# One 33-row matmul in place of two one-row matmuls in the first expert's weight fold

## The chip, the cores and the metric
The kernel runs on one core of one Trainium2 chip. The metric is the device time of one execution in microseconds (us); the time before is the median of three runs. The engines are PE (matrix multiply; PEld is its weight load), DVE (vector), ACT (scalar), POOL (GpSimd) and SP, which here issues the transfers.

## The reference
Two batches of 3008 x 256 go through a two-dimensional Fourier transform, of which the real part is kept; the 6016 rows that come out go through two experts of width 2048, the first with the SiLU activation, the second with a leaky ramp.

```python
X = np.fft.fft(x, axis=1)
X = np.fft.fft(X, axis=2)
x = X.real.astype(np.float32).reshape(6016, 256)
h = x @ w_in;  g = h * (1.0 / (1.0 + np.exp(-h)))
x = g @ w_out                                          # first expert
h = x @ w_in2; g = np.maximum(h, 0) + alpha * np.minimum(h, 0)
return g @ w_out2                                      # second expert
```

## The kernel before
The transform along the 256 columns is not done on the data. It is folded into the first expert's input weights: each of four groups g of 512 weight columns is made ready in two halves h, and in each half sums and differences of weight rows are multiplied by a cosine and a sine table. The products with the table rows take full precision by splitting numbers: a value is held as a high part, which the engine's rounded float keeps exactly, and a low part, the rest.

The half h of a group g goes through seven steps in `prep_w1`. `total` and `rest` (DVE, L436 and L439) form sums and differences in a tile `we`, 256 columns each: the left half is called even, the right half odd. `high` (ACT, L442) copies all 512 columns to `WI[1, g, 2h]`, rounded. `low` (DVE, L446) subtracts that from `we` and writes the low part to `WI[1, g, 2h + 1]`. `fold` (PE, L459) issues eight matmuls of 256 columns into one PSUM bank `cw`: five for the even output (cosine table high times even high and even low, cosine table low times even high, and two more for the odd row) and three for the odd output. The two for the odd row have one partition each: row 0 of the odd half, high and then low, against a table row `OD0` that holds 0, 1, 0, 1, ... . `fold_high` (ACT, L469) and `fold_low` (DVE, L475) read the bank back into `WI`, split again.

Group 0 is made in an opening section whose order on every engine is written out by hand. Groups 1 to 3 are made inside the main loop of the first expert, while it already runs: the dictionary `PLAN` gives the iterations in which their steps are traced (i1 and f1 for group 1, and so on; i holds the steps up to `low`, f those from `fold` on). In that part the order of instructions in each engine's queue is chosen when the program is built, by a list scheduler that simulates the engines' times; `leash` holds the planned steps of an iteration behind named instructions of the iterations just before it on the same engine. The last part, the second expert, again has an order written by hand.

An iteration of the main loop multiplies the transformed data by 128 weight columns. `eo_half` (PE, L627 to L629) makes `pe` and `po`, three matmuls of 502 columns each; DVE adds and subtracts them (`t` at L642, `hp` at L645, `t` at L646); ACT takes the SiLU twice for each (L651, L652); POOL or DVE makes the low part (L664); and three iterations later `mm2` (PE, L686 to L690) multiplies by the output weights. `pe`, `po` and the fold's `cw` all come out of one pool of four PSUM banks, taken in turn: a bank of `po` is free again after L646, a bank of `cw` after L475. A second pool of four banks holds the sums of `mm2`, which ACT (L699) and DVE (L697, L695) carry out when a pass over a block ends.

Of the kernel before, what the change touches and what calls it, by code (L numbers as in the profile page):

```python
# [9 lines left out]
F32 = mybir.dt.float32  # L10
F32R = mybir.dt.float32r
# [60 lines left out]
def _tables():  # L72
    c = np.zeros((128, NCONST), np.float64)
    n1 = np.arange(N1)
    th = 2 * np.pi * np.outer(n1, np.arange(33)) / N1
    fa = np.zeros((N1, 64))
    fa[:, :32] = np.cos(th[:, :32])
    fa[:, 32] = np.cos(th[:, 32])
    fa[:, 33:] = np.sin(th[:, 1:32])
    fr = fa.copy()  # L80
    fr[:, 1:32] = -fa[:, 33:]
    fr[:, 33:] = fa[:, 1:32]
    for q in range(2):
        for j in range(2):
            for k0, k1 in zip(K_PARTS, K_PARTS[1:]):
                at = 4 * k0 + (2 * q + j) * (k1 - k0)
                for to, f in ((FA0, fa), (FR0, fr)):
                    c[64 * q : 64 * q + 64, to + at : to + at + k1 - k0] = f[:, 32 * j + k0 : 32 * j + k1]
    n2 = np.arange(24)
    ph = 2 * np.pi * np.outer(n2, np.arange(N2)) / N2  # L90
    co, si = np.cos(ph), np.sin(ph)
    row = 4 * (n2 % 12) + 2 * (n2 // 12)
    for h, (re, im) in enumerate(((co, -si), (si, co))):
        for j in range(2):
            for to, at in ((R0 + 94 * h, 47 * j), (RS0 + 95 * h, 48 if j else None)):
                if at is None:
                    c[row, to : to + 24] = re[:, :24]
                    c[row + 1, to + 24 : to + 48] = re[:, :24]
                else:
                    c[48 * j + row, to + at : to + at + 47] = re  # L100
                    c[48 * j + row + 1, to + at : to + at + 47] = im
    m = np.arange(128)
    ps = 2 * np.pi * np.outer(m, m) / D
    c[:, CD0 : CD0 + 128] = np.cos(ps)
    c[0, CD0 : CD0 + 128] = c[:, CD0] = 1 - m % 2
    c[:, SD0 : SD0 + 128] = -np.sin(ps)
    c[0, SG0 : SG0 + 128] = 1
    c[:, OC0 : OC0 + 2] = (m % 2)[:, None]
    c[0, OD0 : OD0 + 128] = m % 2
    return c.astype(np.float32)  # L110


# [11 lines left out]
def fft_moe_kernel(  # L124
# [32 lines left out]
    def mm_ps(name, w=512):  # L157
        return pm.tile([128, w], F32, tag="mm", name=name)
# [234 lines left out]
    WS = {}  # L393
    RAW = {}
    TOP = []

    def load_part(key, src, at, o, w):

# [25 lines left out]
    def prep_w1(g):  # L424

        pieces = []

        def steps(h, v):
            t = []
            ps = []  # L430

            def total(eng):
                if h == 0:
                    wi_tiles(1, g)
                t.append(conv(F32, f"we{g}_{h}"))
                eng.tensor_tensor(t[0][:, :256], v[0][:, :256], v[0][:, 256:], op=ALU.add)  # L436

            def rest(eng):
                eng.tensor_tensor(t[0][:, 256:], v[0][:, :256], v[0][:, 256:], op=ALU.subtract)  # L439

            def high():
                nc.scalar.activation(WI[1, g, 2 * h], t[0], AF.Copy)  # L442

            def low(eng):
                hi, lo = WI[1, g, 2 * h], WI[1, g, 2 * h + 1]
                eng.tensor_tensor(lo, t[0], hi.bitcast(F32), op=ALU.subtract)  # L446

            def fold():
                e, o = ([WI[1, g, 2 * h + j][:, at : at + 256] for j in range(2)] for at in (0, 256))
                ps.append(mm_ps(f"cw{g}_{h}"))  # L450
                runs = (
                    ((ch, CD0, e[0]), (ch, CD0, e[1]), (cl, CD0, e[0]), (ch, OD0, o[0]), (ch, OD0, o[1])),
                    ((ch, SD0, o[0]), (ch, SD0, o[1]), (cl, SD0, o[0])),
                )
                for k, run_ in enumerate(runs):
                    for j, (w, at, x) in enumerate(run_):
                        w = w[:, at - CD0 : at - CD0 + 128]
                        to = ps[0][:, 256 * k : 256 * k + 256]
                        nc.tensor.matmul(to, w, x, start=j == 0, stop=j == len(run_) - 1)  # L459
                if g:  # L460
                    return
                ps.append(acc_ps(f"r{g}_{h}", 4))
                for q in range(2):
                    for j in range(2):
                        w = e[j][:, 128 * q : 128 * q + 128]
                        nc.tensor.matmul(ps[1][:, 2 * q : 2 * q + 2], w, co, start=j == 0, stop=j == 1)

            def fold_high():
                nc.scalar.activation(WI[1, g, 2 * h], ps[0], AF.Copy)  # L469
                if g == 0:  # L470
                    nc.scalar.activation(odd_sb[:, 2 * h : 2 * h + 2], ps[1][:, ::2], AF.Copy)

            def fold_low():
                hi, lo = WI[1, g, 2 * h], WI[1, g, 2 * h + 1]
                nc.vector.tensor_tensor(lo, ps[0], hi.bitcast(F32), op=ALU.subtract)  # L475

            return [lambda: total(nc.vector), lambda: rest(nc.vector), high, (lambda: low(nc.vector)), fold, fold_high, fold_low]

        for h in range(2):
            v, st = to_f32(None, (f"i{g}", 512 * h, 512), f"i{g}_{h}")  # L480
            pieces.append((st, steps(h, v)))
        return pieces
# [392 lines left out]
    if True:  # L875
        with tc.manual_schedule():
            zero = conv(F32, "zero")
            nc.vector.memset(zero[:, :256], 0.0)
            warm(zero[:, :128], zero[:, :256], WARM0)
            for j in range(2):  # L880
                TOP.append(xp.tile([128, 512], U32, tag="xs", name=f"top{j}"))
                nc.gpsimd.memset(TOP[j].bitcast(F32), 0.0)
            nc.vector.memset(sm, 0.0)
            nc.scalar.activation(sm[:1, :1], sm[:1, :1], AF.Silu)
            for j in range(len(PIECES) - 1):
                load_x(0, j, (PIECES[j + 1] - PIECES[j]) // 2)
                if j == 0:
                    nc.sync.dma_start(cs[:, :R0], cst[:, :R0])
            cc = conv(F32, "cc")
            load_half("i0", wi1, 0)  # L890
            nc.sync.dma_start(cc, cst[:, CD0:])
            load_half("i0", wi1, 1)
            nc.sync.dma_start(cs[:, R0:], cst[:, R0:CD0])
            fold, mm, rest = stage_a(0)
            (i00, post0), (i01, post1) = prep_w1(0)
            post0, post1 = ([s if callable(s) else s[1] for s in p] for p in (post0, post1))
            for (h, i), n in zip(A_ORDER, A_WARM):
                if h == 0:
                    run(fold(i))
                mm(h, i)  # L900
                warm(cs[:, FA0 : FA0 + 128], cs[:, :256], n)
            for h in range(2):
                load_y(0, h, 0)
            load_half("o0", wo1, 0)
            rest(1)
            load_half("o0", wo1, 1)
            for h in range(2):
                load_y(0, h, 1)
            rest(2)
            load_w1(1)  # L910
            for h in range(2):
                load_y(0, h, 2)
            load_o1(1)
            nc.sync.dma_start(alpha_sb, alpha)
            (s0, p0), (s1, p1) = prep_o1(0)
            warm(cs[:, FA0 : FA0 + 128], cs[:, :256], WARM[0])
            run(i00[:1])
            nc.scalar.activation(ch, cc, AF.Copy)
            run(i00[1:])
            run(post0[:2])  # L920
            nc.vector.tensor_tensor(cl, cc[:, : SG0 - CD0], ch.bitcast(F32)[:, : SG0 - CD0], op=ALU.subtract)
            nc.gpsimd.tensor_copy(co, cs[:, OC0 : OC0 + 2])
            run(post0[2:4])
            run(i01)
            run(post1[:2])
            run(post0[4:5])
            warm(cs[:, FA0 : FA0 + 128], cs[:, :256], WARM[1])
            run(post0[5:])
            run(post1[2:4])
            warm(cs[:, FA0 : FA0 + 128], cs[:, :256], WARM[2])  # L930
            b00, b01 = stage_b(0, 0), stage_b(0, 1)
            run(b00[:2])
            run(b01[:2])
            run(s0)
            ps0 = eo_mm(0, lambda: first_row(0, 0))
            run(post1[4:5])
            ps1 = eo_mm(1)
            run(p0[:1])
            silu_split(0, *ps0, between=lambda: run(post1[5:]))
            run(p0[1:])  # L940
            silu_split(1, *ps1)
# [181 lines left out]
```

## Time and profile before

| what | value |
|---|---|
| median of three runs | 949.72 us (949.55 to 949.81) |
| the profiled execution | 950.28 us, of which the span from first to last instruction is 947.9 us |
| PE busy | 938.3 us (99%) |
| DVE, ACT, POOL busy | 740.9 us (78%), 709.2 us (75%), 368.5 us (39%) |
| granted TensorE clock, mean | 0.999 of 2.4 GHz |

A busy share says how much of the span an engine had an instruction under way; PE's matmuls overlap in it, so a matmul's own duration is longer than the step to the next one. Where an engine sat idle, the trace names what ended the wait; that name is inferred from the last event before the start.

### The profile page before, as it was taken

How to read it: one execution, taken by the hardware profiler on the slowest of the kernel's cores; microseconds unless marked ns; L12 is line 12 of the kernel's file. 1: busy time of each engine (PE TensorE's matmuls, PEld its weight loads, DVE VectorE, ACT ScalarE, POOL GpSimd, SP SyncE). 2: the span in 40 equal slices, each digit the busy share in tenths (PEclk: the TensorE clock that was granted, in tenths of full speed). 3: DMA queues.
4: the chain of work that ended last, by engine and by line, in shares of the span. 5: the costliest groups of instructions: out<-in, count | busy, mean ns of one | idle time of the engine just before them, and what ended most of it. 6: DMA issues, size and time to landing. Idle time of an engine off the chain costs nothing.

```text
span 947.9 us, 14357 instructions
## 1 busy us (share of the span) xinstructions
PE 938.3 (99%) x5188; PEld 816.0 (86%) x5188; DVE 740.9 (78%) x1277; ACT 709.2 (75%) x1398; POOL 368.5 (39%) x324
## 2 busy tenths in 40 slices
PE   8999999999999999999999999999999999999997
PEld 5888888888888888888899999999999999999996
DVE  5898988977756566786988788787888878788876
ACT  4777776755766676776978888787888878788875
POOL 2356658732466666876422122121212212121200
PEclk9999999999999999999999999999999999999999
DMA  8730300134303311100200200020020002000000
GB/s 270 266 99 22 131 28 23 67 82 143 124 1 117 133 59 42 44 1 1 87 22 2 66 1 23 1 67 22 1 66 1 22 2 66 23 1 22 1 23 22
DMA packets 18638, 51.98 MB, mean 55 GB/s; under 512 B 1924, under 2 KB 11912, under 8 KB 16392
## 3 DMA queue, kind: packets, MB, share of 16 engines
q1 hardware_dynamic: 18568, 51.08, 16.0%
q8 instruction: 40, 0.66, 0.3%
q14 instruction: 30, 0.25, 0.1%
HBM read 35.58 MB, written 15.49 MB: 54 GB/s over the span
## 4 chain that ended last, share of the span: by engine, by line
PE 95%; DVE 2%; ACT 1%; issue 1%; DMA 0%; POOL 0%; SPq 0%; ACTq 0%; DVEq 0%
PE a L858 27%; PE ac L760 21%; PE a L686 9%; PE a L688 9%; PE a L690 9%; PE b L760 3%; PE pe L627 2%; PE pe L629 2%; PE pe L628 2%; PE po L629 2%; PE po L628 2%; PE po L627 2%; PE psb L338 1%; PE psa L284 1%; PE cw L459 1%
## 5 line engine op out<-in xcount | busy, mean ns | idle before, releaser
L858 PE MATMUL a<-gh,wo 128*128 128x502 f32 x768 | 267.7, 390 | 0.0
L858 PEld LDWEIGHTS a<-gh,wo 128*128 128x128 f32 x768 | 144.7, 188 | 22.7
L664 POOL TENSOR_TENSOR gl<-t,gh 128x502 fp32r<-128x502 f32 x96 | 126.8, 1321 | 81.5 <-ACT t L652 66.4
L827 DVE SCALAR_TENSOR_TENSOR h<-h,fc,q 128x502 f32<-128x502 f32 x192 | 125.0, 651 | 34.4 <-ACT q L822 30.3
L858 PE MATMUL a<-gl,wo 128*128 128x502 f32 x384 | 149.5, 390 | 0.0
L838 DVE TENSOR_TENSOR gl<-h,gh 128x502 fp32r<-128x502 f32 x192 | 144.9, 755 | 0.1
L651 ACT ACTIVATE gh<-hp 128x502 fp32r<-128x502 f32 x96 | 59.8, 623 | 98.8 <-DVE hp L645 97.3
L688 PE MATMUL a<-gl,wo 128*128 128x502 f32 x384 | 129.9, 391 | 0.0
L690 PE MATMUL a<-gh,wo 128*128 128x502 f32 x384 | 128.1, 390 | 0.0
L686 PE MATMUL a<-gh,wo 128*128 128x502 f32 x384 | 125.0, 391 | 0.0
L833 ACT ACTIVATE gh<-h 128x502 fp32r<-128x502 f32 x192 | 118.4, 617 | 2.2 <-DVE h L827 2.1
L822 ACT ACTIVATE q<-h,fc 128x502 f32<-128x502 f32 x192 | 116.8, 609 | 2.8 <-DVE h L805 1.5
L664 POOL TENSOR_TENSOR gl<-hp,gh 128x502 fp32r<-128x502 f32 x63 | 81.5, 1294 | 81.5 <-ACT hp L652 72.5
L642 DVE SCALAR_TENSOR_TENSOR t<-n,sm,pe 128x502 f32<-128x502 f32 x96 | 70.3, 732 | 48.5 <-PE pe L629 40.1
L690 PEld LDWEIGHTS a<-gh,wo 128*128 128x128 f32 x384 | 72.4, 189 | 15.0
L688 PEld LDWEIGHTS a<-gl,wo 128*128 128x128 f32 x384 | 72.3, 189 | 14.9
L746 POOL TENSOR_TENSOR os<-o1r,os 128x252 fp32r<-128x252 f32 x36 | 33.1, 930 | 132.4 <-ACT os L745 132.4
L686 PEld LDWEIGHTS a<-gh,wo 128*128 128x128 f32 x384 | 71.8, 189 | 14.2
L858 PEld LDWEIGHTS a<-gl,wo 128*128 128x128 f32 x384 | 72.4, 188 | 7.7
L794 ACT ACTIVATE u<-ac 128x252 f32<-128x252 f32 x96 | 36.6, 382 | 54.2 <-PE ac L760 54.1
L736 POOL TENSOR_TENSOR xt<-o1r 128x252 f32<-128x252 f32 x24 | 17.4, 728 | 153.8 <-DVE h L827 150.2
L645 DVE TENSOR_TENSOR hp<-t,po 128x502 f32<-128x502 f32 x96 | 64.6, 673 | 14.2 <-PE po L629 9.6
(162 smaller groups left out, 2187.8 us busy)
## 6 DMA issues: line engine op xcount, KB each, us to landing
od<-o SPq DMA_DIRECT2D x6, 1004.0 KB, 4.3
o1r<-od SPq DMA_DIRECT2D x6, 1004.0 KB, 5.7
out_t<-ot SPq DMA_DIRECT2D x24, 251.0 KB, 2.6
x<-in_xs SPq DMA_DIRECT2D x8, 512.0 KB, 6.5
raw_w<-in_wi SPq DMA_DIRECT2D x4, 1024.0 KB, 8.0
raw_w<-in_wo SPq DMA_DIRECT2D x4, 1024.0 KB, 7.5
raw_i<-in_wi SPq DMA_DIRECT2D x3, 1024.0 KB, 5.8
raw_o<-in_wo SPq DMA_DIRECT2D x3, 1024.0 KB, 6.7
```

What stands on the lines that cost most here:

```text
L642: nc.vector.scalar_tensor_tensor(t, E128[c], odd_sb[:, f : f + 1], pe, op0=ALU.mult, op1=ALU.add)
L645: nc.vector.tensor_tensor(hp, t, po, op=ALU.add)
L664: LAST["gl", i] = (nc.gpsimd if s or lo_pool(i + 1) else nc.vector).tensor_tensor(lo, h, hi.bitcast(F32), op=ALU.subtract)
L686: nc.tensor.matmul(ACC1[lb, s], hi, G[i, s][0], start=st, stop=False)
L688: nc.tensor.matmul(ACC1[lb, s], hi, G[i, s][1], start=False, stop=False)
L690: nc.tensor.matmul(ACC1[lb, s], lo, G[i, s][0], start=False, stop=sp)
L760: nc.tensor.matmul(to, w, x, start=start and q == 0, stop=q == 2, skip_group_check=True)
L822: nc.scalar.activation(h["q", i][:, to], source(n, part), AF.Abs, scale=coef(n, i, 1))
L827: nc.vector.scalar_tensor_tensor(h[f"h{i}"][:, to], source(n, part), coef(n, i, 0), h["q", i][:, to], op0=ALU.mult, op1=ALU.add)
L833: nc.scalar.activation(hi, H[n][f"h{i}"], AF.Copy)
L838: nc.vector.tensor_tensor(lo, H[n][f"h{i}"], G[n, i][0].bitcast(F32), op=ALU.subtract)
L858: nc.tensor.matmul(ACC2[lb], w[lb][j], x, start=st and first, stop=sp and last)
```

## The change
For groups 1 to 3 the two one-row matmuls become one matmul of 33 rows. Two new tiles `PAIR` (33 partitions x 256, one for each half h, kept for the whole kernel) hold the high part of the odd row in partition 0 and its low part in partition 32; the rows between are zero. The table row `OD0` is repeated in partition 32 of the constants. `high` gets a second ACT copy of one partition x 256, `low` a second DVE subtraction of one partition x 256, both written to `PAIR`; both are done six times. The two tiles are set to zero by POOL at the start. Group 0 keeps its two matmuls.

```diff
@@ _tables
-    c[0, OD0 : OD0 + 128] = m % 2
+    c[0, OD0 : OD0 + 128] = c[32, OD0 : OD0 + 128] = m % 2
@@ fft_moe_kernel
     TOP = []
+    PAIR = []
@@ prep_w1
             def high():
                 nc.scalar.activation(WI[1, g, 2 * h], t[0], AF.Copy)
+                if g:
+                    nc.scalar.activation(PAIR[h][:1], t[0][:1, 256:], AF.Copy)
 
             def low(eng):
                 hi, lo = WI[1, g, 2 * h], WI[1, g, 2 * h + 1]
                 eng.tensor_tensor(lo, t[0], hi.bitcast(F32), op=ALU.subtract)
+                if g:
+                    eng.tensor_tensor(PAIR[h][32:33], t[0][:1, 256:], hi.bitcast(F32)[:1, 256:], op=ALU.subtract)
 
             def fold():
                 e, o = ([WI[1, g, 2 * h + j][:, at : at + 256] for j in range(2)] for at in (0, 256))
                 ps.append(mm_ps(f"cw{g}_{h}"))
+                if g:
+                    first = ((ch[:33], OD0, PAIR[h]),)
+                else:
+                    first = ((ch[:1], OD0, o[0][:1]), (ch[:1], OD0, o[1][:1]))
                 runs = (
-                    ((ch, CD0, e[0]), (ch, CD0, e[1]), (cl, CD0, e[0]), (ch, OD0, o[0]), (ch, OD0, o[1])),
+                    ((ch, CD0, e[0]), (ch, CD0, e[1]), (cl, CD0, e[0]), *first),
                     ((ch, SD0, o[0]), (ch, SD0, o[1]), (cl, SD0, o[0])),
                 )
@@ the opening section
             for j in range(2):
                 TOP.append(xp.tile([128, 512], U32, tag="xs", name=f"top{j}"))
                 nc.gpsimd.memset(TOP[j].bitcast(F32), 0.0)
+                PAIR.append(wp.tile([33, 256], F32R, name=f"pair{j}"))
+                nc.gpsimd.memset(PAIR[j].bitcast(F32), 0.0)
```

## Rows read from the trace of the kernel before

**Rows 1.** The profile's first part: busy time, share of the span, instructions.
```profile
PE 938.3 (99%) x5188; PEld 816.0 (86%) x5188; DVE 740.9 (78%) x1277; ACT 709.2 (75%) x1398; POOL 368.5 (39%) x324
```

**Rows 2.** Who PE waited for, whole span; in total, times, longest.
```profile
PE cw L459 <- ACT wi L442: 0.5, 1, 0.5
PE cw L459 <- ACT o L699: 0.5, 1, 0.5
PE cw L459 <- DVE wi L446: 0.3, 1, 0.3
```

**Rows 3.** Busy time by engine from 30 to 155 us: stretch, length, busy.
```profile
30.00:155.00 125.00, 124.53 (x591) 104.42 (x589) 110.44 (x161) 93.74 (x167) 76.56 (x60) 1.00 0.27 92
```

**Rows 4.** PE in order of time: start, us; first fold matmul, first instruction after.
```profile
139.86 0.40 PE L459 MATMUL cw<-wi,ch 128*128 128x256 f32 x2
...
140.79 0.39 PE L686 MATMUL a<-gh,wo 128*128 128x502 f32 x1
```

**Rows 5.** The fold's line, 60 to 150 us: duration min/median/max in ns.
```profile
L459 PE MATMUL cw<-wi,ch x36: 277/280/356, 65.8 to 146.1; 128*128 128x256 f32 x36
```

**Rows 6.** DVE on the tile we, all groups: duration min/median/max in ns.
```profile
L436 DVE TENSOR_TENSOR we<-cvi x8: 418/664/1504, 18.4 to 135.3; 128x256 f32<-128x256 f32 x8
L439 DVE TENSOR_TENSOR we<-cvi x8: 411/417/419, 18.7 to 136.1; 128x256 f32<-128x256 f32 x8
...
L446 DVE TENSOR_TENSOR wi<-we,wi x8: 679/776/1486, 19.9 to 137.8; 128x512 fp32r<-128x512 f32 x8
```

**Rows 7.** DVE groups by shape: busy us, mean ns; the narrowest subtraction.
```profile
L358 DVE TENSOR_TENSOR z<-psb,z 128x63 fp32r<-128x63 f32 x4 | 0.9, 214 | 0.0
```

**Rows 8.** DVE in order of time, three instructions without a wait between them.
```profile
92.47 0.42 DVE L436 TENSOR_TENSOR we<-cvi 128x256 f32<-128x256 f32 x1
92.80 0.42 DVE L439 TENSOR_TENSOR we<-cvi 128x256 f32<-128x256 f32 x1
93.14 0.73 DVE L642 SCALAR_TENSOR_TENSOR t<-n,sm,pe 128x502 f32<-128x502 f32 x1
```

**Rows 9.** ACT groups by shape: busy us, mean ns.
```profile
L169 ACT ACTIVATE xr<-x 128x256 fp32r<-128x256 f32 x4 | 1.6, 403 | 0.0
...
L884 ACT ACTIVATE sm<-sm 1x1 f32<-1x1 f32 x1 | 0.2, 202 | 0.0
```

**Rows 10.** All engines in order of time around group 1's second fold; idle in brackets.
```profile
64.15 1.41 DVE L446 TENSOR_TENSOR wi<-we,wi 128x512 fp32r<-128x512 f32 x1 [0.93 <-ACT wi L442]
...
65.30 0.63 ACT L652 ACTIVATE hp<-hp 128x502 f32<-128x502 f32 x1
...
65.48 0.67 DVE L646 TENSOR_TENSOR t<-t,po 128x502 f32<-128x502 f32 x1
...
66.00 1.27 POOL L664 TENSOR_TENSOR gl<-hp,gh 128x502 fp32r<-128x502 f32 x1 [0.99 <-ACT hp L652]
...
66.07 1.75 DVE L194 SCALAR_TENSOR_TENSOR cvt<-raw_t,top 128x512 uint32<-128x512 uint32 x1
...
70.13 0.39 PE L629 MATMUL po<-z,wi 128*128 128x502 f32 x1
70.18 0.66 DVE L646 TENSOR_TENSOR t<-t,po 128x502 f32<-128x502 f32 x1
70.27 0.57 ACT L699 ACTIVATE o<-a 128x502 f32<-128x502 f32 x1
...
70.99 0.47 PE L459 MATMUL cw<-wi,ch 128*128 128x256 f32 x2 [0.47 <-ACT o L699]
```

**Rows 11.** All engines in order of time around group 2's second fold.
```profile
115.76 0.66 DVE L646 TENSOR_TENSOR t<-t,po 128x502 f32<-128x502 f32 x1
...
118.62 0.40 PE L459 MATMUL cw<-wi,ch 128*128 128x256 f32 x2
```

**Rows 12.** POOL in order of time at the start; idle before in brackets.
```profile
0.71 0.99 POOL L882 MEMSET top<- 128x512 f32 x2 [0.29 <-POOLq L1105]
6.65 1.77 POOL L256 TENSOR_TENSOR x<-x 128x512 f32<-128x512 f32 x1 [4.95 <-DVE x L256]
```

## The prediction, made before the changed kernel was run
> **What bounds the kernel now.** I read the profile's first part, then PE's list of waits, then the stage in which the edit lies, and last the instructions around the edit in order of time. The first part shows PE busy for 938.3 of 947.9 us, with DVE next at 740.9 [rows 1]: time is PE's, and a change pays only in matmul time removed or in waits of PE. Of the waits that concern the fold there are three [rows 2]; two of them (on L442 and on L446) are group 0's, in the opening section, which the edit leaves alone. The third, 0.47 us, is in group 1's second half. The groups that change are made between 30 and 155 us, and there PE is busy 124.53 of 125.00 us: the missing 0.47 is this one wait. But DVE is busy 110.44 us in it and ACT 93.74 [rows 3], so DVE, which gets extra work, has 14.6 us free in the stage, far less headroom than its 78% of the whole span suggests.
>
> The wait itself: PE issues the last `po` matmul at 70.13 and the fold's first at 70.99, 0.47 us idle [rows 10]. The trace names ACT's L699, which ends at 70.27 + 0.57 = 70.84. DVE's L646 also ends at 70.18 + 0.66 = 70.84. The code decides: L699 frees a bank of the other pool, which the fold does not use, whereas L646 gives back the `po` bank that `cw` needs as the next of four. So PE waited for DVE, and DVE ran from 64.15 with no idle gap of note, one instruction behind another.
>
> **What the change removes.** Six matmuls with their weight loads. A fold is eight matmuls of one shape; from its first to the next instruction's start is 140.79 - 139.86 = 0.93 us [rows 4], so 0.116 us each. The 280 ns that the trace gives one matmul [rows 5] is its own length, overlapped with its neighbours, and is not the price. The two one-row matmuls are recorded in the same form as the 128-row ones [rows 5], and no row shows them cheaper, so the remaining 33-row one is put at 0.116 too. Removed: 6 x 0.116 = 0.70 us. Bounds: 0 if the 33-row one cost as much as the pair, 0.70 if it costs the same as one row.
>
> **What it adds on DVE.** Six subtractions of 256 columns, right behind L446 in the queue. No row shows a one-partition DVE operation. The same 256 columns on 128 partitions take 411 to 419 ns when undisturbed [rows 6]; the narrowest subtraction, 63 columns, takes 214 ns [rows 7]. Width sets the time across these, so I take the 256-column row. In the queue one such instruction moves the next by 92.80 - 92.47 = 0.33 and 93.14 - 92.80 = 0.34 us [rows 8]; I take 0.34, 2.0 us in all. The upper bound comes from L436: up to 1504 ns for the same shape [rows 6], when POOL works at the same time. Rows 10 show how: L194 (two inputs from SBUF) starts at 66.07 inside POOL's 66.00 to 67.27 and ends 0.55 after that. So one subtraction can cost 0.21 to 1.50 us.
>
> At the place that matters the subtraction would start near 65.5, and POOL is idle for the 0.99 us before 66.00 [rows 10], so I leave it at 0.34. Against this stands "SBUF — State Buffer" of the Trainium skill (section "SBUF: two separate sides"): a vector instruction with two SBUF inputs and a GpSimd one that reads SBUF exclude each other, and the later one waits for all of the earlier. The 0.55 us above agrees with it. By it alone, a subtraction that just missed a POOL instruction would be 1.27 us late, and the sum below +1.0 in place of -0.24 (an estimate).
>
> **What it adds on ACT.** Six copies of 256 columns behind L442. The nearest rows are 403 ns (128x256) and 202 ns (1x1) [rows 9]; I take 0.40 as the length, and about 0.31 us as the step to the next, since ACT's neighbours overlap by roughly what DVE's do (an estimate: 0.40 less 0.09). Six give 1.9 us in a stage where ACT has 31 us free [rows 3].
>
> **Where this lands on PE.** In group 1, second half, the subtraction goes between L446 (64.15, 1.41) and L646 (65.48), in a chain that runs to the L646 of 70.18 [rows 10]. There are two ways to the same amount. If DVE alone is late, the chain moves by 0.34, unless L194's wait for POOL swallows it (L194 ends 0.55 after POOL's 67.27 either way). If the ACT copy goes ahead of the SiLUs, L652 (65.30) and with it POOL's 66.00 and the end of L194 move by 0.31. I take 0.34 later for the bank; bounds 0 (swallowed, and the copy behind the SiLUs) and 1.0 (both of group 1's subtractions and a copy arrive: 2 x 0.34 + 0.31). The first fold of group 1 gives 0.116 to PE earlier, but PE then only waits longer at the second: that saving is lost.
>
> In the other folds PE does not wait. The cover there, in group 2's second fold: the `po` bank came free at 115.76 + 0.66 = 116.42 and PE reached the fold at 118.62 [rows 11], 2.2 us later, so 0.34 or 0.5 of lateness is hidden. Should that cover go, each of the five would cost its 0.34.
>
> POOL's two memsets: each between 0.1 and 0.5 us (the 128x512 pair took 0.99), before an idle time of 4.95 us [rows 12]; nothing. No transfer is added or moved. `PAIR` is written again two `PLAN` blocks later, long after its fold has read it; nothing.
>
> **The sum.** -0.70 (six matmuls) + 0.12 (the one saving lost in the wait) + 0.34 (the bank later) = -0.24 us, so 950.28 - 0.24 = 950.04 for a profiled execution. That one stands 0.56 above the median of the runs; against the median it is 949.72 - 0.24 = 949.5 us, -0.03%. A difference below 0.2% (1.9 us) can hardly be told from none.
>
> **The rivals.**
> - *The subtraction is dearer than its width says.* Its output starts in partition 32, all its neighbours' in partition 0. If such an instruction may not overlap its neighbours, it loses the overlap on both sides, 0.09 + 0.08 us by rows 8 (92.47 + 0.42 against 92.80, 92.80 + 0.42 against 93.14): 0.51 in place of 0.34, and the sum is -0.07, 949.65 us. For it: nothing seen; against it: nothing seen. "VectorE: DVE Perf Modes" of the Trainium skill (section "Two Vector instructions with no wait between them") has this as a rule: an instruction whose output starts in another group of 32 partitions than the last one is held until all earlier ones have finished. No row here shows such a case.
> - *DVE becomes the bound in its stage: slower.* At all six places the bank that PE needs next comes late by the subtraction and the copy: 6 x (0.34 + 0.31) - 0.70 = +3.2, 952.9 us. It decides from new waits of 2.6 us together (1.9 + 0.70), 0.43 at each place. For it: DVE 110 of 125 us busy. Against it: one single PE wait in the stage today and 2.2 us of cover at the place looked at.
> - *The queues come out in another order.* The scheduler works from simulated times, and with twelve more and twelve fewer instructions it may interleave differently up to about 460 us. In the good case the 0.47 wait goes too: -0.70 - 0.47 = -1.2, 948.5 us; there is no more PE time to win, so this is a floor. In the bad case two or three waits like the present one appear: -0.24 + 3 x 0.47 = +1.2, 950.9 us.
> - *The change saves nothing on PE*: the 33-row matmul costs as much as the two. Then 949.72 + 0.34 = 950.1 us. Against it: the one-row and the 128-row matmuls of a fold follow one another at one pace.
>
> **How the numbers follow.** Forecast (949.5, own range 949.1 to 949.9) 0.45; dearer subtraction (949.65) 0.20; good order 0.13; bad order 0.09; nothing saved 0.04; DVE as the bound 0.09. From the floor 948.5, less 0.1 for the scatter of the runs, to the bad order's 950.9 with 0.3 of the same: 948.4 to 951.2; only the DVE case and a little of the rest lie outside. Faster than 947.8: 0.03 (the floor lies above it); slower than 951.6: 0.09; within 0.2%: 0.88.
>
> **What the profile after would show.** The fold of groups 1 to 3 with seven matmuls and about 0.81 us from first to next, the removed weight loads with them, 12 PE and PEld records fewer; six 1x256 operations on DVE of about 0.42 us and six on ACT of about 0.40. The wait at the second fold of group 1 is about 0.47 + 0.12 + 0.34 = 0.9 us, and no other PE wait between 30 and 155 us. If the subtraction's neighbours start only at its end, the first rival is right. New PE waits on DVE or ACT in that stage, or matmuls of the iterations in another order, would make the forecast wrong; so would a fold whose seventh matmul takes 0.23 us.

## The result and the profile after

The changed kernel takes 954.62 us in the median (954.15 to 958.96, six runs) and the kernel before beside it 949.63 (948.69 to 950.95, six runs): the ratio is 1.0062 [1.0052, 1.0071]. It is slower, by 5.0 us between the medians (0.6%), and outside the predicted range. The profiled execution took 954.64 us, its span 952.9. Its record shows a granted clock of 0.95, but a matmul of 502 columns lasts 390 ns in it as before, and another execution at a granted clock of 1.0 took 954.88: the clock is not the cause. An execution with a recorded mean clock of 0.993 to 0.996 takes about 4 us longer than one with 0.999 or 1.0 (here the one of 958.96; below four with group 0 alone, three of the whole change in the order of before, and one of 1313.75 us at 0.655 among those of the single 33-row matmul).

Two statements ahead of the result, and with them the title, are not right. The kernel before issues the two odd-row matmuls on all 128 rows, against a table that is zero outside row 0 (that is why [rows 5] show the form 128\*128 alone); they do not have one partition each. And group 0 does not keep them: since row 32 of the table is no longer zero, the change cuts group 0's to one row. So the change is "two 128-row matmuls by one of 33 rows" in groups 1 to 3, and "two 128-row by two 1-row" in group 0.

The first part of the page answers to [rows 1]:

```profile
PE 942.9 (99%) x5182; PEld 816.0 (86%) x5182; DVE 749.2 (79%) x1283; ACT 710.5 (75%) x1404; POOL 368.8 (39%) x326
```

Six matmuls and weight loads are gone, six operations came to DVE and to ACT, two to POOL. PE's busy time grew by 4.6 us all the same (2.1 of it are longer folds, as shown next). The tile `pair`, line by line (duration min/median/max in ns):

```profile
L445 ACT ACTIVATE pair<-we x6: 399/400/401, 56.6 to 141.2; 1x256 fp32r<-1x256 f32 x6
L451 DVE TENSOR_TENSOR pair<-we,wi x6: 415/416/1043, 58.2 to 142.7; 1x256 fp32r<-1x256 f32 x6
L468 PEld LDWEIGHTS cw<-pair,ch x6: 182/183/184, 66.6 to 148.8; 33*128 33x128 f32 x6
L468 PE MATMUL cw<-pair,ch x6: 379/384/385, 66.6 to 148.8; 33*128 33x256 f32 x6
```

The added operations on ACT and DVE have the lengths forecast, but for one subtraction of 1.04 us: it starts at 102.49, inside a POOL instruction that runs from 101.98 to 103.25, the case of the prediction's upper bound. The matmul lasts 384 ns where its 128-row neighbours last 280 [rows 5]. What that means shows in PE's order of time, in group 3's second fold (start, length; [rows 4] has the first one of group 3, the six of the changed kernel take 1.20 to 1.32 us each):

```profile
148.35 0.40 PE L468 MATMUL cw<-wi,ch 128*128 128x256 f32 x2
148.59 0.28 PE L468 MATMUL cw<-wi,cl 128*128 128x256 f32 x1
148.80 0.38 PE L468 MATMUL cw<-pair,ch 33*128 33x256 f32 x1
149.11 0.50 PE L468 MATMUL cw<-wi,ch 128*128 128x256 f32 x2
149.45 0.28 PE L468 MATMUL cw<-wi,cl 128*128 128x256 f32 x1
149.57 0.39 PE L636 MATMUL pe<-z,wi 128*128 128x502 f32 x1
```

Seven matmuls take 149.57 - 148.35 = 1.22 us; eight took 0.93. The step into the 33-row one is 0.21 us, the step out of it 0.31 and the one after that 0.22, instead of 0.117 each. The weight loads of the same stretch show what differs:

```profile
148.48 0.19 PEld L468 LDWEIGHTS cw<-wi,cl 128*128 128x128 f32 x1
148.79 0.18 PEld L468 LDWEIGHTS cw<-pair,ch 33*128 33x128 f32 x1
149.11 0.30 PEld L468 LDWEIGHTS cw<-wi,ch 128*128 128x128 f32 x2
```

Between 128-row matmuls a load starts ahead of its matmul, under the one before (148.48 for the matmul of 148.59). The 33-row load and the next 128-row load start together with their own matmuls (148.79 and 148.80, 149.11 and 149.11), 0.07 us before the recorded end of the matmul in front: most of the overlap is gone on either side. Group 0's one-row pair lengthens its fold in the same way. After, and then before:

```profile
27.53 0.40 PE L468 MATMUL cw<-wi,ch 128*128 128x256 f32 x2
...
27.98 0.93 PE L468 MATMUL cw<-wi,ch 1*128 1x256 f32 x4
...
28.86 0.39 PE L475 MATMUL r<-co,wi 128*128 128x2 f32 x3
```

```profile
27.56 0.40 PE L459 MATMUL cw<-wi,ch 128*128 128x256 f32 x2
...
27.91 0.64 PE L459 MATMUL cw<-wi,ch 128*128 128x256 f32 x4
...
28.50 0.50 PE L466 MATMUL r<-co,wi 128*128 128x2 f32 x4
```

The fold takes 1.33 us in place of 0.94, 0.39 more; it starts 0.03 earlier, so what follows is 0.36 us later.

Next the waits. From 25 to 500 us PE's list holds only these (in total, times, longest):

```profile
PE psa L284 <- DVE t L655: 1.1, 2, 0.9
PE po L636 <- DVE t L655: 1.1, 2, 0.7
```

The waits at the fold are gone from it, that of group 1's second fold [rows 2, 10] too: here four matmuls of `mm2` lie between the `po` product and the fold. In their place PE waits four times for L655, the subtraction that gives a `po` bank back (106.06, 163.90, 168.71 and 180.74 us). The windows show how late in the span that is (stretch, length, busy of PE, PEld, DVE, ACT, POOL); first after, then before:

```profile
30.00:155.00 125.00, 124.46 (x574) 102.53 (x573) 112.21 (x162) 93.90 (x169) 73.19 (x58) 0.95 0.27 92
...
160.00:180.00 20.00, 19.14 (x82) 14.93 (x82) 18.12 (x22) 12.61 (x23) 15.57 (x13) 0.95 0.00 0
180.00:200.00 20.00, 19.05 (x87) 15.56 (x86) 18.70 (x27) 13.86 (x27) 12.40 (x14) 0.95 0.22 79
```

```profile
160.00:180.00 20.00, 20.00 (x89) 16.55 (x88) 19.70 (x28) 15.16 (x27) 17.02 (x14) 1.00 0.11 39
180.00:200.00 20.00, 20.00 (x93) 16.70 (x92) 16.66 (x23) 13.09 (x25) 11.13 (x12) 1.00 0.10 40
```

In the stage where the edit lies PE idles 0.54 us, hardly more than the 0.47 of before [rows 3]; it idles 1.8 us after it, between 160 and 200. The first matmul of `pe` in an iteration, after against before, is 0.36 us late from the second one on (group 0), 1.25 at 62 us, 2.06 at 106, 2.87 at 141, 5.10 at 165 and 5.17 for the last at 433 us. The second expert's length is unchanged. So the whole loss lies between 26 and 190 us.

### The profile page after: what moved, and what is told of

Same layout as the page of the kernel before. It is cut to its first block, busy times and chain, and to the rows that moved or that the text cites. A ratio compares the mean times of both kernels' runs of the same rounds, so it can differ in the third digit from the quotient of the medians.

```text
span 952.9 us, 14360 instructions
## 1 busy us (share of the span) xinstructions
PE 942.9 (99%) x5182; PEld 816.0 (86%) x5182; DVE 749.2 (79%) x1283; ACT 710.5 (75%) x1404; POOL 368.8 (39%) x326
## 4 chain that ended last, share of the span: by engine, by line
PE 88%; DVE 6%; ACT 3%; issue 1%; DMA 0%; POOL 0%; SPq 0%; DVEq 0%; ACTq 0%
PE a L867 27%; PE ac L769 21%; PE a L695 7%; PE a L699 7%; PE a L697 7%; PE b L769 3%; PE pe L636 2%; PE pe L638 2%; PE pe L637 2%; PE po L636 2%; PE po L638 2%; PE po L637 2%; PE psb L338 1%; PE psa L284 1%; ACT gh L660 1%
```

## The experiments

Three batches, each beside runs of the kernel before on the same chip (medians 949.4, 949.25 and 949.33 us). The theories: the matmul's cost on PE; the pair's operations on DVE and ACT; another order of the queues, which the scheduler chose anew. A move of a matmul's start is always that of the same `pe` against the kernel before, in the profiled executions.

**All 128 rows.** The pair has 128 partitions, zero outside rows 0 and 32; group 0 is back at full rows, and also multiplies row 32 by the repeated table row, which changes its weights.

```diff
-first = ((ch[:33], OD0, PAIR[h]),)                       # g > 0
+first = ((ch, OD0, PAIR[h]),)
-first = ((ch[:1], OD0, o[0][:1]), (ch[:1], OD0, o[1][:1]))  # g == 0
+first = ((ch, OD0, o[0]), (ch, OD0, o[1]))
```

> This is the changed kernel with PAIR and its one matmul on 128 partitions (the added rows are zero), and group 0 back at its two matmuls of 128 rows. The order in every queue is that of the changed kernel, instruction for instruction. Theory A (a matmul of another row count costs its weight load twice, going in and coming out): a fold of groups 1 to 3 falls from 1.21 us to 0.82 us, 6 x 0.39 = 2.3 us, and group 0 gives back 0.36 to 0.39 us once or twice: 2.7 us less than the changed kernel, about 952.0 us, still 2.3 us above the kernel before, with the new PE waits on L655 still there. Rival B (row count is not the price, the whole loss is the added work on DVE): no difference to the changed kernel, about 954.6 us. Rival C (the loss is all in the row count): 949 us, as before or below.

954.05 us, ratio 1.0048 [1.0036, 1.0060]. Its queues have exactly the changed kernel's order. Of 5.0 us it gains back 0.3 to 0.6; from the first `pe` to the last it loses 4.84 us instead of 5.20, and the difference is group 0's share. Its folds are short again, but its PE is busy 18.93 us of the stretch from 140 to 160 us where the changed kernel's is 19.93: it waits for DVE instead. The matmul's shape is not where the loss is made in this kernel.

**Group 0 alone.** The kernel before, with one row in group 0's pair.

> The kernel before, with only group 0's two odd-row matmuls cut to one partition; groups 1 to 3 as before, order of all queues as before. Theory A: the second fold of group 0 takes 1.33 us in place of 0.94, and the first pe after it comes 0.36 us later; the first fold stands before a wait that hides it. In all +0.36 us, up to +0.7, so about 950.0 us, a difference at the edge of what five rounds resolve. Rivals B and C as a whole-loss story: B no difference.

950.48 us, 1.0022 [1.0010, 1.0034]. The twelve runs spread from 948.97 to 954.63, four of them above 953, so the trace is the better measure: from the first `pe` to the second the profiled execution loses 0.39 us.

**One 33-row matmul, no pair.** Row 0's high part through `(ch[:33], OD0, o[0][:33])`; the low part of the odd row is left out, as are the operations on DVE and ACT.

> The kernel before, with one matmul of 33 rows on the high part in groups 1 to 3 in place of the two, and no PAIR operations at all; it leaves out the low part of the odd row. Group 0 as before. Theory A: each fold takes 1.21 us in place of 0.93, six times +0.28 = +1.7 us, 951.3 us, plus whatever the changed order of the queues does. Rival B (only the work on DVE and ACT costs): -0.7 us, 948.9 us.

950.04 us, 1.0007 [0.9998, 1.0015], with an order of the queues of its own: with no load on DVE the edit saves nothing; if anything it costs. Its six folds take 1.21 us each, PE waits nowhere between 25 and 500 us, and from the first `pe` to the last it loses 1.35 us, about 6 x 0.28 less the old wait of 0.47.

**The operations alone.** The kernel before, with the copies and subtractions into `PAIR` that nothing reads.

> The kernel before, with PAIR filled as in the change (six copies on ACT, six subtractions on DVE, two memsets) but read by nothing: the fold keeps its two matmuls of 128 rows. Theory A with a second cause in the added work: the six operations and the order that they lead to bring new PE waits, up to +3 us, 952.5 us. If instead these operations are hidden as the prediction had it, +0.3 us, 949.9 us. Its queue order differs from that of both other kernels, so a gain or loss here may also be order alone.

956.56 us, 1.0077 [1.0065, 1.0089]: slower than the whole change. Work that PE doesn't need costs 7.2 us. But it also has an order of its own, so all runs from here on hold the order fixed: each queue's sequence in the planned part is stored, and laid down by edges between neighbours on one engine that order their issue and wait for nothing. The code is shortened:

```diff
+for k, j in zip(order, order[1:]):
+    tc.add_manual_dep(mine[j], mine[k].name, NoSync, reason="fixed order")
```

**The 128-row variant's work in the order of before** (the row-32 term of group 0 as above):

> The work of e1 (PAIR and its matmul on 128 partitions), but every queue of the planned part held in the order of the kernel before by edges that order issue and wait for nothing; the six copies and six subtractions stand right behind L442 and L446. As in e1, group 0 also multiplies row 32 by the repeated table row. Theory A (the loss is the other order of the queues): -0.70 us for the six matmuls and at most 0.5 us back in waits, 949.0 to 949.5 us. Theory B (the loss is the time of the added operations on DVE and ACT, whatever the order): about 954 us, as e1.

951.68 us, 1.0025 [1.0015, 1.0035].

**The work of before in the changed kernel's order**:

> The work of the kernel before, with no PAIR at all and eight matmuls in each fold, but every queue of the planned part held in the order of the changed kernel. Theory A: the loss comes with the order, +4 to +5 us, about 954 us. Theory B: no loss, 949.4 us.

951.36 us, 1.0021 [1.0013, 1.0030]. PE's list of waits from 25 to 500 us has the changed kernel's pattern, without a single added operation:

```profile
PE psa L367 <- DVE t L729: 1.2, 2, 1.0
PE po L710 <- DVE t L729: 0.6, 1, 0.6
```

The two parts add up: 951.68 - 949.25 = 2.4 for the work, 951.36 - 949.25 = 2.1 for the order, and group 0's 0.4 make 4.9 of the 5.0 us. From the first `pe` to the last they are 2.86, 1.83 and 0.39, together 5.08 of 5.20.

**The whole change in the order of before**:

> The changed kernel itself (33 rows, group 0 on one row), every queue of the planned part held in the order of the kernel before. Theory A: with the order restored PE sets the time again and the price of the row count shows in full: a fold of 1.21 us against 0.93 us before, 6 x 0.28 = +1.7 us, and group 0's +0.39 us, so 951.0 to 952.0 us. Theory B: 954.6 us, as the changed kernel.

The median of six is 954.58, ratio 1.0057 [1.0040, 1.0074], but three lie at 952.58 to 952.71 and three at 956.44 to 957.12; the profiled one, 952.66, is read here. It is 3.4 us above before; from first to last `pe` it loses 3.31, of which 0.39 is group 0's, and the 128-row variant in this order loses 2.86. Again the 33 rows cost next to nothing beside the rest.

**The operations alone in the order of before**:

> The work of e4 (PAIR filled and never read, the fold as before), every queue of the planned part held in the order of the kernel before. Theory A: the twelve operations alone cost what the wait at group 1's second fold grows by, +0.3 to +0.9 us, 949.7 to 950.3 us. Theory B: 956.5 us, as e4.

953.14 us, 1.0040 [1.0028, 1.0052]. So of the 7.2 us above 3.9 are the operations and 3.3 the order, by the medians. By the traces only 2.40 of the 3.9 are lost between the first and the last `pe`. About 0.7 is lost at one wait in the second expert, at 517 us, and 0.3 lies outside the span of the instructions; the next run has both too, and what makes them stays open. (The profiled execution of the kernel before is itself 0.5 us longer than its median in this batch, 947.9 us against 947.4 in span.) DVE in order of time, at group 1's first half:

```profile
56.00 1.49 DVE L532 TENSOR_TENSOR wi<-we,wi 128x512 fp32r<-128x512 f32 x1 [0.60 <-ACT wi L526]
57.50 0.41 DVE L534 TENSOR_TENSOR pair<-we,wi 1x256 fp32r<-1x256 f32 x1
57.95 0.68 DVE L734 TENSOR_TENSOR t<-t,po 128x502 f32<-128x502 f32 x1
```

The subtraction (L534) starts when its predecessor has ended (56.00 + 1.49 = 57.49) and its successor starts when it has ended in turn (57.91): no overlap on either side, against 0.09 and 0.08 us in [rows 8].

**The same with the low part written to partition 0** (over the high part; nothing reads the pair):

```diff
-eng.tensor_tensor(PAIR[h][32:33], ...)  # the other arguments stay
+eng.tensor_tensor(PAIR[h][:1], ...)
```

> As e8 (PAIR filled and never read, the fold as before, queues in the order of the kernel before), but the subtraction writes partition 0 in place of partition 32 (over the copy's row, so that PAIR loses it). In e8 DVE falls back behind the kernel before by 0.45 to 0.67 us at each subtraction, 2.9 us after the sixth, and never regains it. Theory A (an instruction whose output starts in another group of 32 partitions overlaps neither neighbour): each subtraction costs 0.34 us, about 0.17 less than in e8, so DVE is 1.7 to 2.0 us late after the sixth and the time is up to 1 us below e8's 953.1 us. Rival (the extra cost is the wait on the rounded copy or the shape): no difference to e8.

951.56 us, 1.0024 [1.0015, 1.0033]: 1.6 us less than with partition 32, 1.3 of it between the first and the last `pe` (1.08 lost in place of 2.40). The same place:

```profile
55.84 1.49 DVE L532 TENSOR_TENSOR wi<-we,wi 128x512 fp32r<-128x512 f32 x1 [0.59 <-ACT wi L526]
57.25 0.41 DVE L534 TENSOR_TENSOR pair<-we,wi 1x256 fp32r<-1x256 f32 x1
57.59 0.66 DVE L734 TENSOR_TENSOR t<-t,po 128x502 f32<-128x502 f32 x1
```

Both overlaps are back, and the step from the subtraction to the next is 57.59 - 57.25 = 0.34. By the ends, it moves DVE by 0.34 where it moved it by 0.54 with partition 32 (57.95 - 57.49 = 0.46, and the lost 0.08). A loss of 951.56 - 949.33 = 2.2 us, 1.08 of it between the first and the last `pe`, remains at the price that the forecast had used.

**One matmul without the operations**, high part only (the low part is left out), on 128 rows and on 33, both in the order of before:

```diff
-first = ((ch, OD0, o[0]), (ch, OD0, o[1]))
+first = ((ch, OD0, o[0]),)            # one kernel
+first = ((ch[:33], OD0, o[0][:33]),)  # the other
```

> The kernel before with only the first of the two odd-row matmuls in groups 1 to 3, on 128 rows, no PAIR operations, queues in the order of the kernel before; it leaves out the low part of the odd row. This is the saving by itself. By the term of the prediction -0.70 us, of which 0.12 is lost in the wait at group 1's second fold: -0.58 us, 948.7 us if before is 949.3.

> As e10, but that one matmul takes 33 rows. Theory: each fold takes 1.21 us where that of e10 takes 0.82, since the weights of another row count are loaded in the open on the way in and out: 6 x 0.39 = 2.3 us more than e10, less up to 0.4 us that the wait at group 1's second fold swallows: about 950.7 us. Rival (row count is free where nothing else waits, as e7 against e5 suggests): the same as e10.

128 rows: 948.60 us, 0.9993 [0.9984, 1.0002]. 33 rows: 950.05, 1.0005 [0.9996, 1.0015]. Both agree with no change within the measurement, but they differ by 1.45 us, with no run of one inside the spread of the other, and the folds show it. 128 rows, then 33 (the x3 of 140.55 is the 33-row matmul with two of 128 rows behind it):

```profile
138.85 0.39 PE L545 MATMUL cw<-wi,ch 128*128 128x256 f32 x2
...
139.66 0.39 PE L772 MATMUL a<-gh,wo 128*128 128x502 f32 x1
```

```profile
140.11 0.40 PE L545 MATMUL cw<-wi,ch 128*128 128x256 f32 x2
140.34 0.28 PE L545 MATMUL cw<-wi,cl 128*128 128x256 f32 x1
140.55 0.81 PE L545 MATMUL cw<-wi,ch 33*128 33x256 f32 x3
141.20 0.28 PE L545 MATMUL cw<-wi,cl 128*128 128x256 f32 x1
141.32 0.39 PE L772 MATMUL a<-gh,wo 128*128 128x502 f32 x1
```

0.81 us against 1.21: six times 0.40 would be 2.4, and the loss from the first `pe` to the last differs by 1.49 (-0.35 and +1.14). The rest falls where PE waits anyway: the wait at group 1's second fold is 0.2 us with 33 rows and 0.6 with 128, and of the 0.62 us that the 128-row kernel has gained by 165 us it loses 0.41 again at the next `po`, whose bank DVE (L732, the L646 of before) has not yet given back.

**The pair by transfers.** The full result, in the order of before: a 128-row pair, filled by twelve transfers of 1 KB from `WI`, with no copy and no subtraction. Row 32 of the table is set by one POOL copy after group 0's folds, so group 0 is as before.

```diff
+for k, x in enumerate((hi, lo)):      # g > 0, shortened
+    nc.sync.dma_start(PAIR[h][32 * k : 32 * k + 1], x[:1, 256:])
+first = ((ch, OD0, PAIR[h]),)         # g > 0
+nc.gpsimd.tensor_copy(ch[32:33, row], ch[:1, row])  # shortened
```

> PAIR on 128 partitions with one matmul of 128 rows, complete and with the reference's result: the two rows are brought from WI by twelve transfers of 1 KB on SP's queue in place of copies and subtractions; the table row is repeated in partition 32 by one POOL copy after group 0's folds; all other queues in the order of the kernel before. If DVE's and ACT's added time is the whole of the loss: the saving of e10, 948.7 us. If the transfers land late for a fold or hold up the weight loads behind them, more than 949.3 us, with a PE wait on a DMA at a fold or an ACT wait at L188.

948.45 us (947.88 to 948.94), 0.9992 [0.9983, 1.0000]: the fastest of all, about 6 us below the change and 0.9 below the kernel before, the latter at the edge of what can be told. (That this run and the 128-row one above, both with the stored order, come out below the kernel before also shows no cost of the edges.) PE's list of waits from 25 to 500 us, and then the pair on PE:

```profile
PE cw L550 <- ACT o L790: 0.6, 1, 0.6
```

```profile
L550 PEld LDWEIGHTS cw<-pair,ch x6: 187/188/188, 65.7 to 144.8; 128*128 128x128 f32 x6
L550 PE MATMUL cw<-pair,ch x6: 277/280/282, 65.8 to 145.0; 128*128 128x256 f32 x6
```

Only group 1's old wait is left, 0.6 us for 0.5. The transfers land 1.6 us after issue in the median, and at least 3.5 us before the matmul that reads them (nine of the twelve have their landing in the trace).

## Why the prediction was wrong

**What bounds the kernel.** That PE's matmul time and waits set the time is right; that one wait in 125 us makes DVE's lateness harmless is not. DVE's 14.6 us of free time [rows 3] are for the greater part (10.7 us by the list of waits) gaps in which it waits for ACT, and ACT waits for DVE in turn. The longest of each in the kernel before, from 30 to 155 us, and then the same three of DVE with the operations alone in the order of before:

```profile
DVE wo L513 <- ACT wo L509: 3.2, 2, 1.9
DVE wi L446 <- ACT wi L442: 2.4, 4, 0.9
DVE cvi L194 <- ACT top L188: 1.9, 2, 1.1
ACT gh L651 <- DVE hp L645: 20.9, 15, 3.1
```

```profile
DVE wo L601 <- ACT wo L597: 3.2, 2, 1.9
DVE wi L532 <- ACT wi L526: 2.4, 4, 0.9
DVE cvi L277 <- ACT top L271: 1.9, 2, 1.1
```

With more work on DVE these gaps are as long as before, only later: an added operation moves the gap along instead of filling it.

**"0.34 or 0.5 of lateness is hidden"** is the step that failed. The 2.2 us of cover at one place [rows 11] were set against each 0.34 anew, and only folds were looked at. The cover is one stock, and every subtraction draws on it. With the operations alone, in the order of before, L734 (the L646 of before) leads by 0.38 us until the first subtraction; it is then 0.16 late at 58 us, 1.31 at 99, 2.51 at 139, and still 2.49 at 183 us. Two answering rows, of before and of that run:

```profile
138.53 0.67 DVE L646 TENSOR_TENSOR t<-t,po 128x502 f32<-128x502 f32 x1
```

```profile
141.04 0.68 DVE L734 TENSOR_TENSOR t<-t,po 128x502 f32<-128x502 f32 x1
```

That is 0.38 + 2.51 = 2.9 of the 6 x 0.54 = 3.2 us added. Small parts come back on the way (0.28 at L194 near 66 us, which then waits less for POOL), none after the sixth. Where the cover is least is not at a fold, but at a `po` product near 167 us. In the kernel before, and then with the operations alone:

```profile
166.05 0.68 DVE L646 TENSOR_TENSOR t<-t,po 128x502 f32<-128x502 f32 x1
167.10 0.39 PE L627 MATMUL po<-z,wi 128*128 128x502 f32 x1
```

```profile
168.54 0.68 DVE L734 TENSOR_TENSOR t<-t,po 128x502 f32<-128x502 f32 x1
169.28 0.50 PE L715 MATMUL po<-z,wi 128*128 128x502 f32 x1
```

L646 is done at 166.73 and PE begins at 167.10: 0.37 us, not 2.2. The six runs in the order of before that meet this limit put the cover at about 0.2; part of the difference is the weight load of that product, which starts 0.23 us ahead of its matmul in the kernel before (166.87) and together with it when it is late (169.27). Lateness in us against the kernel before, each from its own first `pe`: of DVE at the L646 of 169 us, of PE at the `pe` of 168 us.

| run | DVE | PE |
|---|---|---|
| the whole change | 3.32 | 3.11 |
| 128-row variant | 2.90 | 2.69 |
| operations alone | 2.87 | 2.66 |
| the same on partition 0 | 1.52 | 1.33 |
| one 128-row matmul, no operations | 0.00 | -0.21 |
| pair by transfers | -0.04 | -0.25 |

PE is as late there as DVE less 0.2, whatever the fold's matmuls cost or save: that is why the 33 rows hardly count beside the added operations, and why saving matmuls alone pays so little. Only where PE is later of itself (one 33-row matmul without operations: 1.29 late by 165 us, DVE 0.14) does its own cost stand. How the operations' loss divides between subtraction and ACT's copy was not tried; in the trace with partition 0 DVE's lateness rises by about 0.33 at each of the six subtractions, which speaks for the subtractions.

**The rival "DVE becomes the bound in its stage"** (952.9, chance 0.09) named the right engine and, in the order of before, nearly the size: the whole change costs 3.4 us there, 0.4 of it group 0's, against its 3.2. The agreement in size is partly luck. Its mechanism was wrong in place: not 0.43 at each of six folds, but, with the operations alone, 0.8 us at group 1's second fold and 1.9 at a few bank releases between 136 and 170 us.

**The subtraction's price**: the rival "dearer than its width says" is right, 0.54 us where it put 0.51 and the forecast 0.34. The Trainium skill, "VectorE: DVE Perf Modes" (section "Two Vector instructions with no wait between them"), states that an instruction whose output starts in another group of 32 partitions than the last one's waits until all earlier ones have finished; that concerns L534 and, as its output is back in the first group, the instruction behind it. The two fences with L534 agree. What both missed is that it counts six times: the rival added 0.17 once, and six times 0.2 came out as 1.3 us between the first and the last `pe`.

**The queues in another order** (bad case 950.9, chance 0.09): right that it happens, and 2.1 us in place of 1.4 for the order alone. Four matmuls of `mm2` now precede group 1's second fold, which removes that wait, but the bank releases at 160 to 190 us come late. The forecast's sum had nothing for this. Which of the moved instructions does it was not tried.

**Six matmuls for -0.70.** The sign of this term is wrong for 33 rows: the fold went from 0.93 to 1.22, +0.29 and not -0.116, beyond the term's lower bound of 0 and the rival "saves nothing". The premise that one-row and 128-row matmuls follow one another at one pace came from misreading [rows 5], where all rows are full. With 128 rows the fold is as forecast, 0.81 us, and PE gains 0.62 us by 165 us, of which 0.35 are left at the last `pe`. In the changed kernel the mistake costs little in groups 1 to 3, since PE waits for DVE's banks anyway, and 0.39 us in group 0, which the forecast didn't see.

**What held:** ACT's copy (0.40 long, 0.31 us to the next instruction where that one does not wait), POOL's memsets (304 ns each, at 1.2 and 1.9 us, nobody waiting), and the wait at group 1's second fold in the order of before, forecast at 0.9; it is 1.0 with the whole change and 1.2 with the operations alone.

## What to carry to other kernels

Cover in front of the bounding engine is a stock, not an allowance for each place: add up all that an edit puts on the engine behind it, ask where that engine would ever catch up, and look for the smallest cover downstream, also beyond the edit's own stage. A matmul was cheapest here in the shape of its neighbours; cutting its rows cost time, so pad with zeros. If small rows must be moved between partitions and there is time for it to land, try a transfer. When a scheduler orders the queues, time the old work in the new order before blaming the work.

## What the runs showed of the hardware

- A matmul with fewer rows than its neighbours, here 33 or 1 against 128, loses most of the overlap of its own weight load and of the next one's: steps of 0.21, 0.31 and 0.22 us in place of 0.117 with 33 rows, and 0.39 us more for a fold with two of one row. The load itself is hardly shorter, 183 ns against 188: the Trainium skill says so too ("TensorE: Matmul & The Clock Gate", section "LDWEIGHTS (loading the stationary operand)": its time goes by the columns, not by the rows).
- A DVE subtraction of one partition x 256 takes 415 ns, as long as one of 128 partitions [rows 6].
- Its output in partition 32, between neighbours that write from partition 0, costs DVE 0.54 us in place of 0.34.
- A transfer of 1 KB from one tile to another lands 1.6 us after issue in the median, 3.2 at most.
